# Decode attention on one core: the value product takes four cache rows per instruction in two column groups instead of two rows in four, for fourteen of sixteen V tiles

## The chip, the cores and the metric

The kernel runs on one core of a Trainium2 chip. Its time is the device time of one execution in microseconds (us); beside it stands the span of one profiled execution, from its first to its last instruction. Engines: PE (TensorE matmul; PEld is its weight load), DVE (VectorE), ACT (ScalarE), POOL (GpSimd), SP (SyncE, which here only issues DMAs). A line number like L491 is a line of the kernel.

## The reference

One decode step of a transformer block for 8 sequences, model width 512, float32 throughout. A modulation of six vectors per sequence comes from `silu(c) @ w_mod`. Attention has 32 query heads of width 128 over 8 cached heads, so 4 query heads share a K and a V; it sees the last 2048 of 8192 cached positions.

```python
W = min(4096, max(256, Sk // 4))                     # 2048
q = (x @ wq).reshape(B, Sq, Hq, Dh).transpose(0, 2, 1, 3)
k = repeat(k_cache[:, :, Sk - W:, :], 4, axis=1)
v = repeat(v_cache[:, :, Sk - W:, :], 4, axis=1)
p = softmax(einsum("bhqd,bhkd->bhqk", q, k) * Dh ** -0.5)
o = einsum("bhqk,bhkd->bhqd", p, v)
attention = o.transpose(0, 2, 1, 3).reshape(B, Sq, Hq * Dh) @ wo
...
h = layernorm(x) * (1 + ca) + sa
x = x + ga * attention(h)
h = layernorm(x) * (1 + cb) + sb
h = h @ w1 + b1;  h = max(h, 0) ** 2                 # 512 -> 1792
x = x + gb * (h @ w2 + b2)                           # 1792 -> 512
```

## The kernel before, in words

**Loads.** The cache is read once, in 32 tiles of 4 MB: K and V of each of 8 heads, each in two tiles. Together with the weights some 164 MB pass through SP's DMA queue, in an order written out by hand (`loads`): w_mod, wq, the first K tiles, then K tile n and V tile n - 2 in turn, with the pieces of `wo` between them, and at the end V14, V15, `tail` (the last of `wo` and half of w1), the rest of w1, and w2. There are four big slots in SBUF (`home`) and one small one. `load` gives a tile the slot that came free first; `done(key)` frees a slot after the last instruction that reads it, and `pump` then issues the next load.

**The loop.** All engines' instructions are put out in the order of the program (a manual schedule). The stage loop counts s from 0 to 37. Head g has four stages (i = s mod 4). A stage handles half a K tile, and half a V tile five stages behind (`PV_LAG`, v = s - 5). Its steps:

- `transposes` (L234, DVE): 32x32 blocks of K turned into `kT`, four calls a stage. `scores` (L405, PE): four instructions 32 outputs wide, one in each column group of TensorE, 512 columns each.
- `soft_a` to `soft_g`: when a head's scores are complete, the maximum (`mx`, a product with the identity in L421, `m`), a permutation by a product (`p_ps`, L436), the negative maximum (L441, `nm`), the exponential on ACT (L448), its multiplication by masks into `pr4` (L454 on ACT, L464 on DVE), and the transpose into `pT` (L471), which the value products use as weights. L477 (`pz`) sums the denominators.
- `weighted(v, h)` (L491, PE): a quarter of a V tile. V tile n covers one head hk and four of the eight sequences; its 16 KB per partition hold 64 cache rows j of 128 values. The weights are 16 columns for a row j (four sequences by four query heads). One instruction takes two rows, so 32 output partitions by 256 columns, of which the blocks with equal row on both sides are wanted; four instructions fill the four column groups, and twice that makes a quarter of the tile. Four quarters add up in one PSUM tile `o_ps`; the last of them frees the V tile.
- `parts(n)` (L508, L509, DVE): of the 2 x 2 blocks the wanted ones are picked by the masks `bit[4]` and added into `o_sb`, in two operations.
- `gather(hk)` (L526, PE, 64 outputs wide): the products with `pick` add up over partitions, put the heads in order, and DVE (L528, L532) writes them as columns to `oT`.
- `project_o(j)` (L544, PE): every second head, `wo` is applied to `oT` and added in `wo_ps`. For j = 0 and 1 one eighth of the rows of `wo` (the "far" rows, those whose index leaves 7 when divided by 8 and are not read with the others) comes by an indirect DMA in another order; there four products with `fsel` (L555), one for each r, bring the matching rows of `oT[:, 7]` into that order, ACT copies them to `oX`, and `far_rows` (L565) uses them four stages or so later.

The masks are made at the start from the identity: `bit[k]` is one bit of the partition number, `own` has four columns, one for each value of bits 2 and 3.

**The end.** After the last stage come `project_o(3)`, the residual and layer norm, w1 (L688), the squared ReLU, and w2 (L707), each waiting for its weights. `spin` (L643) puts products without a use on PE. In the last head's `soft_g` ACT issues five loads of the biases b1 and b2 (L580).

Of the kernel before, what the change touches and what calls it, by code (L numbers as in the profile page):

```python
# [8 lines left out]
F32 = mybir.dt.float32  # L9
AF = mybir.ActivationFunctionType  # L10
ALU = mybir.AluOpType
AX = mybir.AxisListType
# [8 lines left out]
def tile_adaln_cached_attention_mlp(  # L21
# [14 lines left out]
    nc = tc.nc  # L36
    P = 128
    B, HKV, SK, DH = k_cache.shape
# [15 lines left out]
    consts = ctx.enter_context(tc.tile_pool(name="consts", bufs=1))  # L54
    work = ctx.enter_context(tc.tile_pool(name="work", bufs=2))
# [10 lines left out]
    for q in range(D // P):  # L66
        b = slice(32 * q, 32 * q + B)
        nc.scalar.dma_start(xc_in[b], xc[b])

    ident = consts.tile([P, P], F32, name="ident")  # L70
# [2 lines left out]
    nc.gpsimd.memset(ones, 1.0)  # L73
    eps = consts.tile([P, 1], F32, name="eps")
    nc.vector.memset(eps, EPS)
    fsel = consts.tile([P, 4, P], F32, name="fsel")
    oX = consts.tile([P, 8, 32], F32, name="oX")
    pieces = consts.tile([P, 2], mybir.dt.int32, name="pieces")

# [2 lines left out]
    ways, n = [], 0  # L82
    for m, k in GROUPS:
        h, q = divmod(n, 4)
# [12 lines left out]
    nc.vector.tensor_copy(pieces[:, 0:1], pr_[:, 0:1])  # L97
    nc.vector.tensor_scalar(pieces[:, 1:2], pr_[:, 0:1], 2.0 * P, None, op0=ALU.add)
    nc.gpsimd.memset(fsel, 0.0)
    for to, h, q in ways:  # L100
        nc.gpsimd.tensor_copy(fsel[:, :, to], ident.rearrange("p (h r q) -> p r h q", h=8, r=4)[:, :, h, q])

# [76 lines left out]
    def slot(key, n, o=0):  # L181

        t = slots[size_of(key)][held[key]][:, o:]
        return t[:, : t.shape[1] // n * n].rearrange("p (a n) -> p a n", n=n)
# [16 lines left out]
    def done(*keys):  # L201
        for k in keys:
            free[size_of(k)].append(held.pop(k))
        pump()
# [39 lines left out]
    e = work.tile([P, P], F32, name="e_sb", tag="one_e_sb", bufs=1)  # L244
# [34 lines left out]
    h = work.tile([P, P], F32, name="h_sb", tag="one_h_sb", bufs=1)  # L279
# [5 lines left out]
    bit = {}  # L285
    for k in (2, 3, 4):
        n = 1 << k
        bit[k] = consts.tile([P, 2], F32, name=f"bit{k}")
        tmp = work.tile([P, 32 // n], F32, name=f"tmp{k}")
        nc.vector.tensor_reduce(tmp, sel[:, :32].rearrange("p (a n) -> p a n", n=n), axis=AX.X, op=ALU.add)  # L290
        nc.vector.tensor_reduce(bit[k], tmp.rearrange("p (a x) -> p x a", x=2), axis=AX.X, op=ALU.add)

    own = consts.tile([P, 4], F32, name="own")
    bq = consts.tile([P, B], F32, name="bq")
    for x in range(2):
# [16 lines left out]
    oT = consts.tile([P, 8, 32], F32, name="oT")  # L312
# [4 lines left out]
    for i, last in enumerate((16, 8)):  # L317
        at_ = 0
        while at_ < last:
            kc, m = divmod(16 * i + at_, 6)  # L320
            n = min(4 - m if m < 4 else 6 - m, last - at_)
            wv = slot(("mod", i), D)[:, at_ : at_ + n].rearrange("p m (q n) -> p m q n", q=NQ)
            for q in range(NQ):
# [4 lines left out]
                    start=(kc == 0),  # L328
                    stop=(kc == NQ - 1),
# [16 lines left out]
    for kc in range(NQ):  # L346
        w = slot(("wq", kc // 2), 512)[:, kc % 2 * 8 : kc % 2 * 8 + 8]
        for r in range(2):
            for g in range(4):
# [4 lines left out]
                    start=(kc == 0),  # L354
                    stop=(kc == NQ - 1),
# [21 lines left out]
    PT_, RZ_, RZP_, OS_, O_, MX_, SS_, X_ = {}, {}, {}, {}, {}, {}, {}, {}  # L377
# [90 lines left out]
    def soft_g(hk):  # L468
# [8 lines left out]
        nc.tensor.matmul(pz[b, :B], tsel.rearrange("p t d -> p (t d)"), RZP_.pop(hk), start=True, stop=True)  # L477
        nc.vector.reciprocal(RZ_[hk][b], pz[b, :B])

    def weighted(v, h):  # L480


        n, f = v // 2, 2 * (v % 2) + h
        hk, e = divmod(n, 2)
        vt = slot(("V", n), DH)
        if f == 0:
            O_[n] = ps_o.tile([P, 512], F32, name="o_ps")
        for x in range(2):
            for g in range(4):
                j = 16 * f + 8 * x + 2 * g  # L490
                nc.tensor.matmul(  # L491
                    O_[n][32 * g : 32 * g + 32, : 2 * DH],
                    PT_[hk][:, e, j : j + 2].rearrange("p j r -> p (j r)"),
                    vt[:, j : j + 2, :].rearrange("p j d -> p (j d)"),
                    start=(f == 0 and x == 0),
                    stop=(f == 3 and x == 1),
                )
        if f == 3:
            done(("V", n))

    def parts(n):

        hk, e = divmod(n, 2)
        o = O_.pop(n)
        if e == 0:
            OS_[hk] = work.tile([P, 2, P], F32, name="o_sb", bufs=1)
        d = OS_[hk][:, e, :]
        nc.vector.tensor_scalar(d, o[:, :DH], bit[4][:, 0:1], None, op0=ALU.mult)  # L508
        nc.vector.scalar_tensor_tensor(d, o[:, DH : 2 * DH], bit[4][:, 1:2], d, op0=ALU.mult, op1=ALU.add)  # L509

    def gather(hk):

# [25 lines left out]
    def project_o(j):  # L538

        last = j == HKV // 2 - 1  # L540
        key = ("tail", 0) if last else ("wo", j)
        w = slot(key, D)
        for i in range(8 if j > 1 else 7):
            nc.tensor.matmul(  # L544
                wo_ps[32 * (i % 4) : 32 * (i % 4) + 32, :],
                oT[:, i, :],
                w[:, i, :],
                start=(j == 0 and i < 4),
                stop=(last and i >= 4),
            )  # L550
        if j < 2:

            px = ps_m.tile([P, 512], F32, name="m_ps", tag="m_ps")
            for r in range(4):
                nc.tensor.matmul(px[:, 32 * r : 32 * r + 32], fsel[:, r], oT[:, 7, :], start=True, stop=True)  # L555
            px = px[:, :P].rearrange("p (r b) -> p r b", b=32)
            nc.scalar.copy(oX[:, :4], px)
        if not last:
            done(key)
# [26 lines left out]
    for s in range(N + PV_LAG + 1):  # L586
        g, i = divmod(s, C)
        q, h = divmod(s, 2)
# [15 lines left out]
        if v > C and v % (2 * C) == 1 and v < N:  # L604
            project_o(v // C // 2 - 1)
        if s in (18, 25):
            far_rows(s // 25)
        if 1 <= v <= N:
            weighted(v - 1, 1)
# [10 lines left out]
        if 1 <= v <= N and v % 2 == 0:  # L620
            parts(v // 2 - 1)
# [8 lines left out]
        if 0 <= v < N:  # L630
            weighted(v, 0)
        if ends:
            gather(v // C - 1)

    project_o(HKV // 2 - 1)


# [41 lines left out]
    for kc in range(NQ):  # L679
# [7 lines left out]
        for g in range(NQ):  # L687
# [4 lines left out]
                start=False,  # L692
                stop=(kc == NQ - 1),
# [3 lines left out]
    r = work.tile([P, FC, B], F32, name="relu", tag="a", bufs=1)  # L697
# [7 lines left out]
    for f in range(FC):  # L705
        for q in range(NQ):
# [4 lines left out]
                start=False,  # L711
                stop=(f == FC - 1),
            )
    y = work.tile([P, P], F32, name="y", tag="one_e_sb", bufs=1)
# [39 lines left out]
```

## Time and profile before

| | |
|---|---|
| time of three runs | 392.83, 392.85, 392.96 us; median 392.85 |
| profiled execution | span 390.9 us; its own time is not recorded beside it, the runs' median is 1.95 us longer |
| PE busy | 260.2 us (67%), of it L405 129.0 us, L491 68.5 us |
| DVE busy | 224.2 us (57%), of it L234 151.4 us |
| HBM read | 166.24 MB, 425 GB/s over the span |
| granted TensorE clock | 0.900 of full speed, mean |

A matmul in float32 shows as two records in the trace, so the 512 instructions of L491 count as 1024. A row of the timeline has start, duration, engine, line, operation, tile written <- tiles read, shape, count, and in brackets the engine's idle time before it and what ended that. Several rows of PE overlap, because a record lasts until its modelled end; the time that a step takes is read from start to start. A row of the windows view has busy time and count for each engine, then the granted clock (PEclk), the DMA engines' busy share and the GB/s.

### The profile page before, as it was taken

The numbers are of one execution on the slowest core, as the hardware profiler recorded it, in microseconds if no ns is written. First come the engines' busy times: TensorE is split into PE (matmuls) and PEld (weight loads), VectorE is DVE, ScalarE is ACT, GpSimd is POOL, SyncE is SP. The second block draws the span as 40 slices with busy tenths as digits, with TensorE's granted clock in tenths as the row PEclk, the third lists the DMA queues.
The fourth block names the chain that finished last, engine by engine and source line by source line (L and its number), as shares of the span: only waits on it lengthen the run. The fifth ranks groups of instructions, "written<-read, shape, count | busy, mean of one in ns | idle before, by whom it ended". The sixth has DMA issues, their size and how long they took to land.

```text
span 390.9 us, 4829 instructions
## 1 busy us (share of the span) xinstructions
PE 260.2 (67%) x2066; PEld 81.8 (21%) x2066; DVE 224.2 (57%) x316; ACT 46.7 (12%) x91; POOL 10.2 (3%) x36
## 2 busy tenths in 40 slices
PE   0080958868337973798379737783788237996895
PEld 0030211112011321242113212321222011322433
DVE  1360099879057935775579457391789057855231
ACT  0120011221003100310031003100201003004010
POOL 4000000000000000030000000200000000000000
PEclk9997789999859996999599969989799859998999
DMA  8999999999999999999999999999999999999995
GB/s 330 431 436 423 434 443 436 438 426 403 441 429 429 431 433 433 431 438 419 431 424 433 431 443 423 428 433 428 433 428 419 443 436 428 425 433 420 416 433 224
DMA packets 7157, 165.04 MB, mean 422 GB/s; under 512 B 1016, under 2 KB 1184, under 8 KB 1440
## 3 DMA queue, kind: packets, MB, share of 16 engines
q1 hardware_dynamic: 6768, 164.17, 98.1%
q0 software_dynamic: 288, 0.53, 0.4%
q8 instruction: 16, 0.26, 0.3%
q10 hardware_dynamic: 80, 0.04, 0.0%
q14 instruction: 5, 0.04, 0.0%
HBM read 166.24 MB, written 0.07 MB: 425 GB/s over the span
## 4 chain that ended last, share of the span: by engine, by line
DMA 53%; DVE 23%; PE 18%; issue 5%; ACT 1%; SPq 0%; ACTq 0%; DVEq 0%
DMA home<-in_A_k_cache_dram 37%; DVE kT L234 12%; DMA home<-in_A_wq_dram 9%; PE s_ps L405 6%; DMA home<-in_B_w_dram 5%; DVE pT L471 5%; PE p_ps L436 3%; PE o_ps L491 3%; PE m_ps L350 2%; DVE pr L464 2%; DMA pr<-in_B_b_dram 2%; DVE mx L419 1%; PE m_ps L421 1%; DVE qbd L368 1%; PE m_ps L441 1%
## 5 line engine op out<-in xcount | busy, mean ns | idle before, releaser
L234 DVE STREAM_TRANSPOSE kT<-home 128x1024 f32<-128x1024 f32 x128 | 151.4, 1220 | 79.7 <-DMA home<-in_A_k_cache_dram 75.8
L405 PE MATMUL s_ps<-kT,qst 128*32 128x512 f32 x512 | 129.0, 1075 | 12.2 <-DVE kT L234 11.9
L491 PE MATMUL o_ps<-home,pT 128*32 128x256 f32 x1024 | 68.5, 390 | 10.8 <-DVE pT L471 10.5
L491 PEld LDWEIGHTS o_ps<-home,pT 128*32 128x32 f32 x1024 | 33.2, 115 | 101.1 <-issue 57.8
L421 PE MATMUL m_ps<-ident,mx 128*1 128x128 f32 x16 | 4.3, 364 | 63.8 <-DVE mx L419 63.8
L405 PEld LDWEIGHTS s_ps<-kT,qst 128*32 128x32 f32 x512 | 14.1, 114 | 30.5 <-DVE kT L234 22.4
L471 DVE STREAM_TRANSPOSE pT<-pr 128x2048 f32<-128x2048 f32 x8 | 18.3, 2281 | 1.0 <-ACT pr L454 1.0
L454 ACT ACTIVATE pr<-pr,own 128x512 f32<-128x512 f32 x16 | 17.8, 1225 | 0.3
L448 ACT ACTIVATE pr<-p_ps,nm 128x512 f32<-128x512 f32 x8 | 5.5, 688 | 102.7 <-DVE nm L445 102.7
L350 PE MATMUL m_ps<-home,oX 128*32 128x512 f32 x64 | 9.5, 757 | 9.8 <-DMA home<-in_A_wq_dram 9.8
L415 ACT COPY ss<-s_ps 128x512 f32<-128x512 f32 x8 | 4.7, 586 | 90.5 <-issue 62.4
L421 PEld LDWEIGHTS m_ps<-ident,mx 128*1 128x1 f32 x16 | 0.7, 81 | 69.0 <-DVE mx L419 69.0
L393 ACT COPY qst<-q_ps 32x128 f32<-32x128 f32 x32 | 8.2, 257 | 52.2 <-PE q_ps L382 52.0
L368 DVE COPY qbd<-m_ps 32x128 f32<-32x128 f32 x8 | 3.0, 373 | 18.8 <-PE m_ps L365 18.7
L436 PE MATMUL p_ps<-ss,perm 128*128 128x512 f32 x16 | 12.9, 896 | 0.0
L445 DVE TENSOR_SCALAR nm<-m_ps 128x1 f32<-128x1 f32 x8 | 1.3, 159 | 17.5 <-PE m_ps L441 17.5
L268 PE MATMUL m_ps<-xsum,sel 128*128 128x1 f32 x2 | 0.6, 363 | 15.5 <-DVE xsum L266 15.5
L526 PE MATMUL m_ps<-o_sb,pick 128*64 128x224 f32 (+2 forms) x48 | 9.9, 345 | 0.9 <-DVE o_sb L509 0.9
L154 POOL MEMSET small<- 128x2048 f32 x2 | 3.6, 1802 | 240.8 <-PE wo_ps L544 240.8
L464 DVE TENSOR_SCALAR pr<-pr,own 128x512 f32<-128x512 f32 x16 | 9.2, 661 | 0.8 <-ACT pr L448 0.8
L528 DVE STREAM_TRANSPOSE tr<-m_ps 64x512 f32<-64x512 f32 x8 | 5.7, 714 | 5.5 <-PE m_ps L526 5.2
L508 DVE TENSOR_SCALAR o_sb<-o_ps,bit 128x128 f32<-128x128 f32 x16 | 5.3, 329 | 4.7 <-PE o_ps L491 4.5
(139 smaller groups left out, 137.7 us busy)
## 6 DMA issues: line engine op xcount, KB each, us to landing
home<-in_A_k_cache_dram SPq DMA_DIRECT2D x16, 4096.0 KB, 31.1
home<-in_A_v_cache_dram SPq DMA_DIRECT2D x15, 4096.0 KB, 20.6
home<-in_w_mod_dram SPq DMA_DIRECT2D x1, 4096.0 KB, 12.7
home<-in_A_v_cache_dram SPq DMA_DIRECT2D x2, 2048.0 KB, 19.5
small<-in_A_wo_dram SPq DMA_DIRECT2D x2, 1792.0 KB
small<-in_w_mod_dram SPq DMA_DIRECT2D x1, 2048.0 KB
small<-in_A_wo_dram SPq DMA_DIRECT2D x1, 2048.0 KB
home<-in_A_wo_dram SPq DMA_DIRECT2D x1, 2048.0 KB, 14.6
```

The lines of the kernel that those rows point to most:

```text
L234: nc.vector.transpose(KTS[q, j][:, rows], k[:, rows, 32 * j : 32 * j + 32])
L350: nc.tensor.matmul(pqs[r][32 * g : 32 * g + 32, :], hT[:, kc, :], w[:, 4 * r + g, :], start=(kc == 0), stop=(kc == NQ - 1),)
L368: nc.vector.tensor_copy(qbd[b, 4 * r : 4 * r + 4, j].rearrange("p g (b t) -> p t g b", t=REP), pT_[b].rearrange("p (t g b) -> p t g b", t= ...
L393: nc.scalar.copy(own[b, :, :, i, 0], pq[b, :P].rearrange("p (c m t) -> p c m t", c=2, t=REP))
L405: nc.tensor.matmul(s_ps[0][32 * g : 32 * g + 32, :], qst[hk % 2][:, P * (4 * c + u) + 32 * j :][:, :32], kT[:, u], start=(c == 0 and j == ...
L421: nc.tensor.matmul(MX_[hk][0:1, :P], mx, ident, start=True, stop=True)
L436: nc.tensor.matmul(sp, perm, SS_.pop(hk), start=True, stop=True)
L454: nc.scalar.mul(X_[hk][..., w], pr, own[:, w : w + 1])
L464: nc.vector.tensor_scalar(X_[hk][..., w], pr, own[:, w : w + 1], None, op0=ALU.mult)
L471: nc.vector.transpose(PT_[hk].rearrange("p e j r -> p j e r"), X_.pop(hk).rearrange("p j x w -> p j (x w)"))
L491: nc.tensor.matmul(O_[n][32 * g : 32 * g + 32, : 2 * DH], PT_[hk][:, e, j : j + 2].rearrange("p j r -> p (j r)"), vt[:, j : j + 2, :].rear ...
L526: nc.tensor.matmul(dest, pick[:, x].rearrange("p t u -> p (t u)"), src, start=True, stop=True)
```

## The change

For V tiles 0 to 13 (`at_once(n)` is 4, for 14 and 15 it stays 2) an instruction of `weighted` takes four cache rows: 64 output partitions by 512 columns, in two column groups of 64. A quarter of a tile is then four instructions instead of eight. Of the 4 x 4 blocks four are wanted, so `parts` uses four masks (`jrow`) and four DVE operations instead of two. The PSUM tile is the same, used in its whole width.

For the far rows, `fsel` no longer has a matrix for each r: it is one 128 x 128 matrix, and `oT[:, 7]` is first copied into four column blocks, each multiplied by the mask of its r (`own`, DVE, into `o7`). One product with 128 columns replaces four with 32. At the start, two reductions for `jrow` and one for `rows_of` are added on DVE, and POOL's copies into `fsel` are a quarter as wide.

```diff
-    fsel = consts.tile([P, 4, P], F32, name="fsel")
+    fsel = consts.tile([P, P], F32, name="fsel")
...
+    rows_of = consts.tile([P, 8, 4], F32, name="rows_of")
+    nc.vector.tensor_reduce(rows_of, ident.rearrange("p (h r q) -> p h q r", h=8, r=4), axis=AX.X, op=ALU.add)
     for to, h, q in ways:
-        nc.gpsimd.tensor_copy(fsel[:, :, to], ident.rearrange("p (h r q) -> p r h q", h=8, r=4)[:, :, h, q])
+        nc.gpsimd.tensor_copy(fsel[:, to], rows_of[:, h, q])
...
+    jrow = consts.tile([P, 4], F32, name="jrow")
+    tmp = work.tile([P, 8], F32, name="tmpj")
+    nc.vector.tensor_reduce(tmp, ident.rearrange("p (a n) -> p a n", n=16), axis=AX.X, op=ALU.add)
+    nc.vector.tensor_reduce(jrow, tmp.rearrange("p (a x) -> p x a", x=4), axis=AX.X, op=ALU.add)
...
+    def at_once(n):
+        return 4 if n < 2 * HKV - 2 else 2
...
+        a = at_once(n)
         for x in range(2):
-            for g in range(4):
-                j = 16 * f + 8 * x + 2 * g
+            for g in range(8 // a):
+                j = 16 * f + 8 * x + a * g
                 nc.tensor.matmul(
-                    O_[n][32 * g : 32 * g + 32, : 2 * DH],
-                    PT_[hk][:, e, j : j + 2].rearrange("p j r -> p (j r)"),
-                    vt[:, j : j + 2, :].rearrange("p j d -> p (j d)"),
+                    O_[n][16 * a * g : 16 * a * (g + 1), : a * DH],
+                    PT_[hk][:, e, j : j + a].rearrange("p j r -> p (j r)"),
+                    vt[:, j : j + a, :].rearrange("p j d -> p (j d)"),
...
-        nc.vector.tensor_scalar(d, o[:, :DH], bit[4][:, 0:1], None, op0=ALU.mult)
-        nc.vector.scalar_tensor_tensor(d, o[:, DH : 2 * DH], bit[4][:, 1:2], d, op0=ALU.mult, op1=ALU.add)
+        row_of = jrow if at_once(n) == 4 else bit[4]
+        nc.vector.tensor_scalar(d, o[:, :DH], row_of[:, 0:1], None, op0=ALU.mult)
+        for x in range(1, at_once(n)):
+            nc.vector.scalar_tensor_tensor(
+                d, o[:, x * DH : (x + 1) * DH], row_of[:, x : x + 1], d, op0=ALU.mult, op1=ALU.add
+            )
...
-            for r in range(4):
-                nc.tensor.matmul(px[:, 32 * r : 32 * r + 32], fsel[:, r], oT[:, 7, :], start=True, stop=True)
+            o7 = work.tile([P, 2, 2, 32], F32, name="o7", bufs=1)
+            nc.vector.tensor_mul(
+                o7,
+                oT[:, 7, None, None, :].to_broadcast([P, 2, 2, 32]),
+                own.rearrange("p (x y) -> p y x", x=2)[..., None].to_broadcast([P, 2, 2, 32]),
+            )
+            nc.tensor.matmul(px[:, :P], fsel, o7.rearrange("p y x b -> p (y x b)"), start=True, stop=True)
```

## The prediction

> **What bounds the kernel now.** I read the page first, then the DMA queue's issues and waits, then the timeline of PE and DVE in the loop and at its end, and the clock by stages.
>
> ```profile
> PE 260.2 (67%) x2066; PEld 81.8 (21%) x2066; DVE 224.2 (57%) x316; ACT 46.7 (12%) x91; POOL 10.2 (3%) x36
> DMA  8999999999999999999999999999999999999995
> DMA 53%; DVE 23%; PE 18%; issue 5%; ACT 1%; SPq 0%; ACTq 0%; DVEq 0%
> ```
>
> The DMA engines are busy in every slice but the first and the last: the stream of loads is the bound, and no engine is. So compute costs nothing while two things hold: slots come free before the stream runs dry, and the work behind the last landings isn't late. The first I read from one head's period, from the landing of one even K tile to the next.
>
> ```profile
> core 0: us, PE busy (x) PEld busy (x) DVE busy (x) ACT busy (x) POOL busy (x), PEclk, DMA share, GB/s
> 189.23:228.55 39.32, 28.25 (x218) 8.64 (x218) 25.54 (x31) 4.62 (x9) 0.00 (x0) 0.89 1.01 433
> ...
> 221.52 1.09 PE L491 MATMUL o_ps<-home,pT 128*32 128x256 f32 x16
> ...
> 228.55 2.37 DVE L234 STREAM_TRANSPOSE kT<-home 128x1024 f32<-128x1024 f32 x2 [9.33 <-DMA home<-in_A_k_cache_dram]
> 316.51 2.37 DVE L234 STREAM_TRANSPOSE kT<-home 128x1024 f32<-128x1024 f32 x2 [14.24 <-DMA home<-in_A_k_cache_dram]
> ...
> 327.88 6.48 SPq L131 DMA_DIRECT2D home<-in_A_v_cache_dram  x2
> 335.86 6.99 DVE L234 STREAM_TRANSPOSE kT<-home 128x1024 f32<-128x1024 f32 x6 [0.74 <-DMA home<-in_A_k_cache_dram]
> ```
>
> In a period of 39.32 us PE works 28.25, is done at 222.6, and DVE then waits 9.33 for the next K tile; K14's landing at 316.51 ends a longer wait, 14.24. V13's load goes out at 327.88, as soon as V11's last product is done, but its turn on the DMA engines comes only when K15 has landed, about 335.9: 8.0 us of slack there.
>
> The second I read from the end.
>
> ```profile
> 354.22 0.25 PE L477 MATMUL m_ps<-zs,tsel 128*64 128x8 f32 x2 [0.58 <-DVE zs L466]
> 357.43 1.86 PE L491 MATMUL o_ps<-home,pT 128*32 128x256 f32 x16 [2.95 <-DVE pT L471]
> 359.22 1.93 PE L526 MATMUL m_ps<-o_sb,pick 128*64 128x256 f32 x4
> 361.08 6.25 PE L491 MATMUL o_ps<-home,pT 128*32 128x256 f32 x112
> ...
> 380.74 1.98 PE L643 MATMUL q_ps<-ident 128*128 128x512 f32 x4
> 383.58 1.96 PE L707 MATMUL m_ps<-home,pr 128*32 128x128 f32 x64 [0.85 <-DMA home<-in_B_w_dram]
> 385.97 1.73 PE L707 MATMUL m_ps<-home,pr 128*32 128x128 f32 x48 [0.44 <-DMA home<-in_B_w_dram]
> ```
>
> From K14's landing to the output there is one long chain of compute beside the stream: softmax of the last two heads, the products of V12 to V15, the output projection, the MLP. It meets the stream again at the last product (L707), which waits for w2 0.85 and 0.44 us. So the chain is only a little early. The spins end at 382.72 as modelled, about 382.5 as the next row would begin; 64 records take 1.96, so 112 take about 3.3, and without a wait PE would be done at 385.8 instead of 387.70. **Slack at the end: 1.9 us.** That is what the change may spend behind K14.
>
> **The change part by part.**
>
> *The product of one quarter V tile* (`weighted`, L491). Before: 8 instructions of 256 columns, 32 outputs wide, so two in each of four column groups. After, for V0 to V13: 4 instructions of 512 columns, 64 wide, so two in each of two groups.
>
> ```profile
> 323.66 1.07 PE L491 MATMUL o_ps<-home,pT 128*32 128x256 f32 x16
> 324.66 0.38 PE L441 MATMUL m_ps<-ones,m 1*128 1x1 f32 x2
> ...
> 332.02 1.07 PE L491 MATMUL o_ps<-home,pT 128*32 128x256 f32 x16 [1.08 <-DVE pT L471]
> 333.02 1.08 PE L526 MATMUL m_ps<-o_sb,pick 128*64 128x256 f32 x4
> ...
> 335.82 1.92 PE L544 MATMUL wo_ps<-small,oT 128*32 128x512 f32 x16
> 337.56 1.04 PE L491 MATMUL o_ps<-home,pT 128*32 128x256 f32 x16
> 338.42 1.98 PE L405 MATMUL s_ps<-kT,qst 128*32 128x512 f32 x8
> 340.20 1.06 PE L491 MATMUL o_ps<-home,pT 128*32 128x256 f32 x16
> 341.09 1.99 PE L405 MATMUL s_ps<-kT,qst 128*32 128x512 f32 x8
> 342.89 1.06 PE L491 MATMUL o_ps<-home,pT 128*32 128x256 f32 x16
> ...
> 345.69 1.07 PE L491 MATMUL o_ps<-home,pT 128*32 128x256 f32 x16
> 346.55 2.01 PE L405 MATMUL s_ps<-kT,qst 128*32 128x512 f32 x8
> 348.34 1.08 PE L491 MATMUL o_ps<-home,pT 128*32 128x256 f32 x16
> 350.04 0.38 PE L421 MATMUL m_ps<-ident,mx 128*1 128x128 f32 x2 [0.61 <-DVE mx L419]
> ```
>
> Start to start the old product takes 0.88 (340.20 to 341.09). L544 streams two 512-column instructions through each of its groups, as the new product will, and takes 1.74 (335.82 to 337.56). It has as many records as the old product (16) and takes twice as long: columns per group set the pace, not the number of instructions. Bounds: 0.44, if half the records meant half the time; about 3.9, if two 64-wide groups did not run side by side (the spins, one stream, take 1.98 for 4 records; here 8). I take 1.74, the row with the same stream per group: **+0.86 per product.** No row has two 64-wide groups at once. The Trainium skill, "TensorEngine Tiling (Array Packing)", Tiling Modes, lists 128x64 as two independent tiles; no run so far shows it.
>
> *Change of width.* Followed by an instruction of the same width (L405) the old product takes 0.88, by one of another (L441, L526) 1.00: 0.12 for a change. The scores stay 32 wide, so a new product between two of them has two changes: 1.74 + 0.24 = 1.98, +1.10. Bounds: 0 and 0.25 each. The Trainium skill, same page, Key Properties, says that a change of tiling mode drains TensorE, which speaks against this change; it gives no time, and the 0.12 agrees. Without that price the sum below would be 1.0 lower.
>
> *Adding the rows up* (`parts`): two more DVE operations for each of 14 tiles.
>
> ```profile
> L509 DVE SCALAR_TENSOR_TENSOR o_sb<-o_ps,bit,o_sb 128x128 f32<-128x128 f32 x16 | 5.6, 351 | 0.6
> ...
> 169.54 4.62 DVE L234 STREAM_TRANSPOSE kT<-home 128x1024 f32<-128x1024 f32 x4 [1.13 <-DMA home<-in_A_k_cache_dram]
> ...
> 169.11 1.92 PE L544 MATMUL wo_ps<-small,oT 128*32 128x512 f32 x14
> 170.96 1.08 PE L555 MATMUL m_ps<-oT,fsel 128*128 128x32 f32 x8
> 171.97 1.07 PE L491 MATMUL o_ps<-home,pT 128*32 128x256 f32 x16
> ```
>
> 2 x 0.35 = 0.70 each, 9.8 in all, in DVE's idle time but for V11 and V13 below.
>
> *Far rows* (`project_o`, twice). Four products (1.01, 170.96 to 171.97) become one, at most 0.38 (L421 has its size), but that waits for a new DVE multiplication (0.35, as L509), queued on DVE behind the first two transposes of an odd K tile (169.54 to 171.9). PE's queue stands meanwhile: the product of a V tile, and through it that tile's release. About 172.7 instead of 172.0, so +0.7 twice (bounds: -0.6, and a late K tile's wait), long before the end; the 8 us of DVE's wait for K covers it. The two setup reductions and the smaller POOL copies lie under the first weight loads; nothing.
>
> *The loop.* Per head the eight products cost PE at most 8 x 1.10 = 8.8. PE would be done at 222.6 + 8.8 = 231.4. What follows on it, L421 for the next head, needs the next K tile's first two transposes (228.55 + 2.37 = 230.9) and a maximum behind them, so it can't come before 231 anyway: it just fits, and the longer wait before K14 clears any rest. A V slot is released 2 us later at 327.88, against 8.0 of slack, so the stream stays whole. The cover is nearly used up: PE's idle time is gone, and any more would move K's release.
>
> *The end.* From K14's landing: the product at 323.66 stands ahead of L441, on which the exponential and pT wait: +0.86. The one at 332.02 is followed by 64-wide L526, so it loses one change: 1.00 to 1.74, +0.74; the two DVE additions (0.70) run beside it. Those at 337.56, 340.20, 342.89 and 345.69 stand in a closed row of PE work: 4 x 1.10 = 4.40. The one at 348.34 had 1.70 until L421 and needs 1.86 to 1.98: +0.2. Both of V13's lie beside the softmax. Sum **6.2**, until pT.
>
> Then a gain. The product at 357.43 and L526 took 3.65 for work that takes 2.0 elsewhere, because the clock had dropped.
>
> ```profile
> 358.00:361.00 3.00, 3.00 (x17) 0.97 (x8) 0.35 (x1) 0.00 (x0) 0.00 (x0) 0.50 1.02 427
> 361.00:364.00 3.00, 3.00 (x57) 1.81 (x60) 0.98 (x3) 0.00 (x0) 0.00 (x0) 1.00 1.01 428
> ...
> 363.31 3.52 SPq L136 DMA_DIRECT2D home<-in_B_w_dram  x4
> ...
> SPq L136 <- DMA pr<-in_B_b_dram: 4.3, 5, 1.6
> ```
>
> PE was idle 2.95 before, with almost nothing (0.25) in the 0.6 before that. V13's two products now last 1.7 longer, so the gap shrinks to about 1.8, between the 1.08 without a drop (332.02) and the 2.95 with one. The Trainium skill, "TensorE: Matmul & The Clock Gate", What's actually happening, has half rate after an idle window of about 3.4 us, free-running; that agrees with the drop here. By it a gap of 1.8 keeps the clock; the sum with a drop would be 0.9 higher. I take no drop. Then L526 waits for V13's four DVE operations instead, and comes at the same distance from pT, but takes 1.0 instead of 1.86: -0.9. **Late by 5.3**, against 1.9 of slack: +3.4. The last weight loads, w2's from 363.31, wait for the bias loads issued behind pT, so they go out some 6 us later; the tail's two pieces (2.1 and 1.8 MB by their shapes) stand ahead of them, 9 us at 430 GB/s. The stream ends when it did; without that cover the end would come up to 6 us later.
>
> The span is 390.9 and the median 392.85, so 1.95 lies around it. 392.85 + 3.4 = 396.25; I say **396.2**.
>
> **The rivals.** *No change, the other side.* The new product takes about as long as the old (0.9 to 1.2, if two wide groups stream faster than L544's four). Then the end is late by some 1.6 at most, under the 1.9, and the time is 392.9: DMA sets it. It decides below a cost of about 0.3 per product. For it: DVE and PE are busy 57% and 67% of the span, under a full stream. Against it: L544's 1.74.
>
> *Wide groups one after another.* A product takes 3.4 to 3.9: +2.6 at least, 20.8 per head on an active part of 33.4 (189.23 to 222.6), so 54 against 39.3. PE is then the bound for seven heads: +15 each, some 105, time 495.
>
> *Faster.* The denser PE keeps its clock and the product is covered; but the end is then w2's landing, 387.3 at the earliest. It needs a faster stream: half a per cent more than some 430 GB/s would be 2 us, 391. The rates of 427 to 433 in the rows above allow for that, and nothing in the change causes it.
>
> **How the numbers follow.** Slower by the end's chain 0.74; its own range is 395.0 (no price for a change of width: 5.3 less 1.0) to 398.3 (0.25 for each change, +1.2, and the clock drops, +0.9). No change 0.14; groups in turn 0.06; faster 0.06. A difference under 0.2% (0.8 us) can't be told from none here. The range 392.7 to 398.3 holds the first two, 0.88. Slower 0.80, same 0.14, faster 0.06.
>
> **What would show it.** After: L491's wide records, 8 per product, in about 1.74; the scores' start-to-start around them 0.24 longer; DVE's waits for K little changed at K10 and K14; PE's idle time before K10 near nothing; DMA in nines; L707 not waiting for w2, its last records ending some 3.4 us after w2's landing plus 0.5; a granted clock near 1.00 after pT of the last head. Wrong if L707 still waits for w2 (then the product was cheap), or if DMA shows holes in the loop (then slots came late).

## The result and the profile after

The changed kernel takes 397.75 us (396.96 to 397.86, 4 runs) against 392.84 (392.66 to 392.96): ratio 1.0122, 95% interval 1.0109 to 1.0134, so **slower by 4.9 us**. The profiled run took 397.78 with a span of 396.0. One of the ten runs of first12, further down, took 816.0 us at a granted clock of 1.00; the record doesn't explain it, and the ratio leaves it out.

The page of the changed kernel, its window over the same period of the loop, and PE's and DVE's timelines there:

```profile
PE 310.7 (78%) x1606; PEld 76.1 (19%) x1606; DVE 236.0 (60%) x349; ACT 46.8 (12%) x91; POOL 9.7 (2%) x36
DMA  8999999999999999999999999999999999999990
DMA 44%; PE 28%; DVE 24%; issue 4%; SPq 0%; ACT 0%; DVEq 0%; ACTq 0%
...
189.23:228.55 39.32, 36.09 (x162) 7.83 (x158) 27.30 (x35) 5.02 (x10) 0.00 (x0) 1.00 1.01 433
...
226.28 1.94 PE L503 MATMUL o_ps<-home,pT 128*64 128x512 f32 x8
231.44 0.48 PE L428 MATMUL m_ps<-ident,mx 128*1 128x128 f32 x2 [3.22 <-DVE mx L426]
...
228.44 2.37 DVE L236 STREAM_TRANSPOSE kT<-home 128x1024 f32<-128x1024 f32 x2 [5.07 <-DMA home<-in_A_k_cache_dram]
316.54 2.37 DVE L236 STREAM_TRANSPOSE kT<-home 128x1024 f32<-128x1024 f32 x2 [10.72 <-DMA home<-in_A_k_cache_dram]
```

The stream of loads is as whole as before: 9 in every slice between the first and the last, 433 GB/s in the period, K10 landing at 228.44 (228.55 before) and K14 at 316.54 (316.51). PE is busy 50 us longer, and nothing of that shows in the loop: the waits for K have shrunk (9.33 to 5.07, 14.24 to 10.72) and PE still idles 3.22 before K10's maximum. But the chain that ended last has shifted from DMA (53% to 44%) towards PE (18% to 28%), and the last slice has a 0 for DMA where it had a 5: the stream is over, and compute ends the kernel.

The end, from K14's landing on (lines have moved: L441 is L448, L526 L542, L421 L428, L477 L484, L491 L503, L405 L412, L544 L560, L707 L728; in the variants further down they move by a few more):

```profile
325.72 0.38 PE L448 MATMUL m_ps<-ones,m 1*128 1x1 f32 x2
334.87 1.03 PE L542 MATMUL m_ps<-o_sb,pick 128*64 128x256 f32 x4
...
339.46 1.94 PE L503 MATMUL o_ps<-home,pT 128*64 128x512 f32 x8
341.33 1.99 PE L412 MATMUL s_ps<-kT,qst 128*32 128x512 f32 x8
343.25 1.94 PE L503 MATMUL o_ps<-home,pT 128*64 128x512 f32 x8
...
354.60 1.94 PE L503 MATMUL o_ps<-home,pT 128*64 128x512 f32 x8
356.46 0.38 PE L428 MATMUL m_ps<-ident,mx 128*1 128x128 f32 x2
361.63 0.23 PE L484 MATMUL m_ps<-zs,tsel 128*64 128x8 f32 x2
361.89 2.31 DVE L478 STREAM_TRANSPOSE pT<-pr 128x2048 f32<-128x2048 f32 x1 [1.39 <-PE m_ps L484]
364.26 1.56 PE L503 MATMUL o_ps<-home,pT 128*32 128x256 f32 x16 [2.40 <-DVE pT L478]
366.03 1.97 PE L542 MATMUL m_ps<-o_sb,pick 128*64 128x256 f32 x4 [0.21 <-DVE o_sb L523]
367.93 6.32 PE L503 MATMUL o_ps<-home,pT 128*32 128x256 f32 x112
387.66 1.98 PE L664 MATMUL q_ps<-ident 128*128 128x512 f32 x4
389.58 3.26 PE L728 MATMUL m_ps<-home,pr 128*32 128x128 f32 x112
```

Read against the same rows of before, the lateness grows like this:

| step | before | after | late by |
|---|---|---|---|
| L441, negative maximum of head 6 | 324.66 | 325.72 | 1.06 |
| L526, gather of head 5 | 333.02 | 334.87 | 1.85 |
| V13's second product, behind the last scores | 348.34 | 354.60 | 6.26 |
| L421, maximum of head 7 | 350.04 | 356.46 | 6.42 |
| first product behind pT | 357.43 | 364.26 | 6.83 |
| the row of seven products | 361.08 | 367.93 | 6.85 |
| spins before w2 | 380.74 | 387.66 | 6.92 |
| PE's end | 387.70 | 392.84 | 5.14 |

The last product no longer waits for w2: its 112 records run in one piece of 3.26. The 6.92 of lateness became 5.14 of time, so 1.78 was slack.

### The profile page after: what moved, and what is told of

It reads as the page before. It is cut to its first block, busy times and chain, and to the rows that moved or that the text cites. A ratio compares the mean times of both kernels' runs of the same rounds, so it can differ in the third digit from the quotient of the medians.

```text
span 396.0 us, 3942 instructions
## 1 busy us (share of the span) xinstructions
PE 310.7 (78%) x1606; PEld 76.1 (19%) x1606; DVE 236.0 (60%) x349; ACT 46.8 (12%) x91; POOL 9.7 (2%) x36
## 4 chain that ended last, share of the span: by engine, by line
DMA 44%; PE 28%; DVE 24%; issue 4%; SPq 0%; ACT 0%; DVEq 0%; ACTq 0%
DMA home<-in_A_k_cache_dram 35%; DVE kT L236 12%; DMA home<-in_A_wq_dram 9%; PE o_ps L503 9%; PE s_ps L412 7%; DVE pT L478 5%; PE p_ps L443 3%; PE m_ps L357 2%; DVE o_sb L523 2%; DVE pr L471 2%; DVE mx L426 1%; PE q_ps L664 1%; PE m_ps L542 1%; PE wo_ps L560 1%; PE m_ps L709 1%
## 5 line engine op out<-in xcount | busy, mean ns | idle before, releaser
L412 PE MATMUL s_ps<-kT,qst 128*32 128x512 f32 x512 | 128.4, 1074 | 5.1 <-DVE kT L236 5.1
L503 PE MATMUL o_ps<-home,pT 128*64 128x512 f32 (+1 forms) x576 | 118.0, 566 | 9.4 <-DVE pT L478 9.4
L503 PEld LDWEIGHTS o_ps<-home,pT 128*64 128x64 f32 (+1 forms) x576 | 31.5, 133 | 131.6 <-issue 106.4
L428 PE MATMUL m_ps<-ident,mx 128*1 128x128 f32 x16 | 3.8, 324 | 28.3 <-DVE mx L426 28.3
L412 PEld LDWEIGHTS s_ps<-kT,qst 128*32 128x32 f32 x512 | 11.4, 112 | 37.4 <-DVE kT L236 19.0
L523 DVE SCALAR_TENSOR_TENSOR o_sb<-o_ps,jrow,o_sb 128x128 f32<-128x128 f32 x42 | 14.7, 351 | 1.5
L443 PE MATMUL p_ps<-ss,perm 128*128 128x512 f32 x16 | 12.0, 843 | 0.0
L542 PE MATMUL m_ps<-o_sb,pick 128*64 128x224 f32 (+2 forms) x48 | 9.8, 342 | 1.1 <-DVE o_sb L523 1.1
L544 DVE STREAM_TRANSPOSE tr<-m_ps 64x512 f32<-64x512 f32 x8 | 5.7, 714 | 4.5 <-PE m_ps L542 4.3
L426 DVE TENSOR_REDUCE mx<-s_ps 128x1 f32<-128x512 f32 x8 | 5.3, 661 | 4.2 <-ACT ss L422 4.2
```

The costliest lines, as they stand in the source:

```text
L412: nc.tensor.matmul(s_ps[0][32 * g : 32 * g + 32, :], qst[hk % 2][:, P * (4 * c + u) + 32 * j :][:, :32], kT[:, u], start=(c == 0 and j == ...
L426: nc.vector.tensor_reduce(mx, s_ps[0], axis=AX.X, op=ALU.max)
L443: nc.tensor.matmul(sp, perm, SS_.pop(hk), start=True, stop=True)
L503: nc.tensor.matmul(O_[n][16 * a * g : 16 * a * (g + 1), : a * DH], PT_[hk][:, e, j : j + a].rearrange("p j r -> p (j r)"), vt[:, j : j + a ...
L523: nc.vector.scalar_tensor_tensor(d, o[:, x * DH : (x + 1) * DH], row_of[:, x : x + 1], d, op0=ALU.mult, op1=ALU.add)
L542: nc.tensor.matmul(dest, pick[:, x].rearrange("p t u -> p (t u)"), src, start=True, stop=True)
```

## The experiments

**Where in the kernel the loss arises.** Two kernels, the wide product for one part of the tiles each.

```diff
-        return 4 if n < 2 * HKV - 2 else 2
+        return 4 if n < 2 * HKV - 4 else 2                       # first12
+        return 4 if 2 * HKV - 4 <= n < 2 * HKV - 2 else 2        # last2
```

> Wide product for V0 to V11 alone; V12 and V13 go back to two rows per instruction. Theory (the loss is PE's row of work behind K14's landing, products of V11 to V13, less the slack of 1.8 us at the end): only V11's last two products are wide behind K14, so the last head's pT comes some 1.2 us later, less than the slack: 392.9 us. Rival (the loss comes from the loop: slots freed later, holes in the stream, twelve fourteenths of the wide products): 397.0 us.

> Wide product for V12 and V13 alone. Theory (end of the kernel): all of the loss but V11's share of 0.9 us: 396.9 us. Rival (loop): two fourteenths of the loss: 393.5 us.

first12: 392.81 us, ratio 1.0004 (0.9994 to 1.0014). last2: 397.91 us (396.07 to 398.56), ratio 1.0138 (1.0121 to 1.0155). Twelve of the fourteen wide tiles by themselves cost nothing, though V11's last two products lie behind K14: the maximum of head 7 comes at 351.24 instead of 350.04, and these 1.20 stay under the slack. The other two tiles cost, by the medians, as much as all. The loop is out. last2 is 1.0 over its forecast, and its four runs lie 2.5 apart. Part of that lies outside the span: the spans are 394.1, 395.5, 395.9 and 395.8 (395.2 to 396.1 for the changed kernel), and two of the four times stand 2.7 above theirs, where the changed kernel's stand 1.8 above. Its profiled run is the one of 396.07:

```profile
319.56 0.37 PE L428 MATMUL m_ps<-ident,mx 128*1 128x128 f32 x1 [13.84 <-DVE mx L426]
321.93 1.12 PE L443 MATMUL p_ps<-ss,perm 128*128 128x512 f32 x2
322.98 1.07 PE L503 MATMUL o_ps<-home,pT 128*32 128x256 f32 x16
354.70 0.38 PE L428 MATMUL m_ps<-ident,mx 128*1 128x128 f32 x2
```

Here p_ps was over in 1.05 (321.93 to 322.98); in the changed kernel it took 1.96 (321.89 to 323.85), at half clock. That 0.9 and V11's 0.87 (its product takes 1.00 until 323.98, in the changed kernel 1.87 until 325.72) make L428 of head 7 1.76 earlier than the changed kernel's 356.46. The other three runs, with no trace, were slower; why they exceed 396.9 stays open.

**The rest of the change by itself.** The change with `at_once` always 2, and for V0 to V13 two more DVE operations in `parts`:

```diff
+        if n < 2 * HKV - 2:
+            d2 = work.tile([P, P], F32, name="d2", bufs=1)
+            for x in range(2):
+                nc.vector.scalar_tensor_tensor(d2, o[:, x * DH : (x + 1) * DH], row_of[:, x : x + 1], d, op0=ALU.mult, op1=ALU.add)
```

> All that the change does but the wide product: the far rows by one product with masked right-hand sides, the masks at the start, and for V0 to V13 two further DVE operations of the same size behind the two (into a tile that nobody reads). Theory: DVE has the idle time, 392.9 us. Rival (the additions and the far rows' wait take part in the loss): 393.6 us or more; V13's additions alone lie on the path to the output and are worth 0.7 us there.

392.73 us, ratio 1.0004 (0.9994 to 1.0013). None of this costs anything. The far rows' wait is there, but covered:

```profile
172.57 0.46 PE L579 MATMUL m_ps<-o,fsel 128*128 128x128 f32 x2 [1.29 <-DVE o L574]
```

One thing this run doesn't test: its further additions write a tile that nobody reads, so V13's gather doesn't wait for them. In the changed kernel it must, which is 0.69 of idle time in keep_clock's rows below. half_columns, next, has the additions on the path.

**Columns or width.** The changed form has twice the columns per group and, against the scores, a change of width. Two kernels have one of them each.

```diff
 half_columns: 64 wide, 256 columns (four additions read the two blocks in turn)
-                    O_[n][16 * a * g : 16 * a * (g + 1), : a * DH],
+                    O_[n][16 * a * g : 16 * a * (g + 1), : 2 * DH],
-                    vt[:, j : j + a, :].rearrange("p j d -> p (j d)"),
+                    vt[:, j : j + 2, :].rearrange("p j d -> p (j d)"),
 double_columns: 32 wide, 512 columns
...
+                m = min(j, 60) if a == 4 else j
                 nc.tensor.matmul(
+                    O_[n][32 * g : 32 * g + 32, : a * DH],
+                    PT_[hk][:, e, j : j + 2].rearrange("p j r -> p (j r)"),
+                    vt[:, m : m + a, :].rearrange("p j d -> p (j d)"),
```

> The wide product with 256 columns instead of 512: 64 wide, two groups, the same number of instructions, half of the columns left out (so half of the wanted blocks are missing), four DVE operations as in the change. Theory (columns per group set the pace, a change of width costs 0.12 us): the product lasts 0.9 and 1.1 between two score products, the last head's pT is late by some 1.3 us, under the slack: 392.9 us. Rival (the 64-wide form itself, its weight loads or the drain at each change of width, is what costs): product stays near 1.9, 397 us.

> Products of V0 to V13 stay 32 wide in four groups, eight instructions a quarter, but each streams 512 columns as the changed kernel's do (the further columns give blocks that nobody wants, so the output isn't the reference's); four DVE operations as in the change. No change of width against the scores. Theory: 1.74 a product, the scores' 1.78 as before; pT of the last head some 1.0 to 1.3 us earlier than in the changed kernel (two changes of width saved at four or five products): 396.6 us. Rival (width costs nothing here, columns all): 397.7 us.

half_columns: 392.91 us, ratio 1.0009 (1.0000 to 1.0019). PE's timeline in the row of products and scores without a pause (337 to 348 us before):

```profile
337.98 1.08 PE L503 MATMUL o_ps<-home,pT 128*64 128x256 f32 x8
338.99 1.98 PE L412 MATMUL s_ps<-kT,qst 128*32 128x512 f32 x8
340.91 1.08 PE L503 MATMUL o_ps<-home,pT 128*64 128x256 f32 x8
```

double_columns: 397.58 us, ratio 1.0118 (1.0101 to 1.0135). The same place:

```profile
341.44 1.98 PE L412 MATMUL s_ps<-kT,qst 128*32 128x512 f32 x8
343.23 1.91 PE L504 MATMUL o_ps<-home,pT 128*32 128x512 f32 x16
344.96 1.98 PE L412 MATMUL s_ps<-kT,qst 128*32 128x512 f32 x8
...
360.95 2.31 DVE L478 STREAM_TRANSPOSE pT<-pr 128x2048 f32<-128x2048 f32 x1 [1.37 <-PE o_ps L504]
363.32 1.07 PE L504 MATMUL o_ps<-home,pT 128*32 128x256 f32 x16 [2.28 <-DVE pT L478]
365.09 1.89 PE L543 MATMUL m_ps<-o_sb,pick 128*64 128x256 f32 x4 [0.70 <-DVE o_sb L524]
```

Start to start, product and scores (256 columns from the kernel before and half_columns, 512 from double_columns and the changed kernel):

| | 32 wide | 64 wide |
|---|---|---|
| 256 columns | 0.88, 1.78 | 1.01, 1.92 |
| 512 columns | 1.73, 1.79 | 1.87, 1.92 |

Columns cost 0.86, a change of width 0.13 on either side, and the two add up. Two groups 64 wide do run side by side: one after another, four streams of 256 columns at 0.43 (half of L544's 0.87 for 512) would take 1.7, not 1.01. The columns are what slows the kernel: the width alone stays under the slack. double_columns has its pT 0.94 before the changed kernel's, about as forecast, but its time of 397.58 is the rival's 397.7, not the forecast 396.6. Its clock drop lay later (granted clock 0.50 from 366 to 368 and 0.85 to 370 us), over part of the seven products: they began 1.02 earlier (366.91 for 367.93), took 7.07 instead of 6.32, and the gather behind them was only 0.26 earlier (374.85 for 375.11).

**The clock drop behind the last scores.** Two spins behind the last L484:

```diff
+        if hk == HKV - 1:
+            gap = ps_1.tile([P, 512], F32, name="q_ps").rearrange("p (a n) -> p a n", a=4)
+            for _ in range(2):
+                nc.tensor.matmul(gap, ident, ident[:, None, :].to_broadcast([P, 4, P]), start=True, stop=True)
```

> The changed kernel with two spins (products without a use, 1.7 us) on PE behind the last head's L484, in the gap of 2.4 us before pT. Theory (the granted clock drops in that gap, so the product behind pT and L542 take 1.56 and 1.97 instead of 1.0 and 1.1): the clock stays at 1.00, L542 begins with the last DVE addition as before and ends 0.9 us sooner: 396.9 us, as the one run of the changed kernel that took 396.96. Rival (those two are slow for another reason): 397.75 us.

396.25 us (395.94 to 396.75), ratio 1.0085 (1.0068 to 1.0102). First two windows of the changed kernel, then one of keep_clock and its PE timeline:

```profile
364.00:366.00 2.00, 1.56 (x16) 0.51 (x16) 1.82 (x6) 0.00 (x0) 0.47 (x1) 0.68 1.00 422
366.00:368.00 2.00, 1.97 (x8) 0.82 (x12) 0.00 (x0) 0.00 (x0) 0.00 (x0) 0.50 1.01 429
```

```profile
364.00:366.00 2.00, 1.28 (x17) 0.61 (x18) 1.61 (x5) 0.00 (x0) 0.47 (x1) 1.00 1.00 422
...
361.56 1.98 PE L489 MATMUL q_ps<-ident 128*128 128x512 f32 x4
364.03 1.07 PE L507 MATMUL o_ps<-home,pT 128*32 128x256 f32 x16 [0.49 <-DVE pT L478]
365.79 1.08 PE L546 MATMUL m_ps<-o_sb,pick 128*64 128x256 f32 x4 [0.69 <-DVE o_sb L527]
366.80 6.25 PE L507 MATMUL o_ps<-home,pT 128*32 128x256 f32 x112
```

With PE busy in the gap the clock stays, and L546 takes 1.01 instead of L542's 1.90. From pT to the seven products it is 5.14 (361.66 to 366.80) instead of 6.04 (361.89 to 367.93): the 0.9 forecast. The time falls by more, 1.5 by the medians; 0.2 of the profiled run's gain had arisen before the spins (its pT began at 361.66), and where the rest comes from isn't shown. In the changed kernel the clock reads 1.00 up to 364, 0.85 in the next microsecond and 0.50 from 365 to 368: it fell only when PE was at work again, not in the gap itself.

**The wait for the old pT.** The last head's pT in the query buffers, which are read out by then:

```diff
+        if hk == HKV - 1:
+            PT_[hk] = qst_all[:, :, : B * P].rearrange("p e (j r) -> p e j r", r=16)
```

> The changed kernel, but the last head's pT lies in a buffer of its own (the query buffers, which are read out by then), so that its transpose doesn't wait until V13's products have read the old pT. Theory: pT begins when ACT is done, 0.4 us earlier: 397.35 us, or 396.5 if the shorter gap of PE (2.0 us) also keeps the clock. Rival (the transpose waits for something else): 397.75 us.

> Both of these at once: pT in a buffer of its own and two spins in the gap. Theory: the two savings add up, 0.4 + 0.9: 396.45 us. What then remains over the kernel before, 3.6, is V11's to V13's products (5.4 by pT) less the slack of 1.8.

own_pT: 397.17 us (396.83 to 399.63), ratio 1.0106 (1.0089 to 1.0123). Its profiled run is the slowest of them, so only its DVE row is used; below it stands the row of the kernel before:

```profile
361.56 2.31 DVE L482 STREAM_TRANSPOSE qst<-pr 128x2048 f32<-128x2048 f32 x1 [1.02 <-ACT pr L462]
...
355.06 2.31 DVE L471 STREAM_TRANSPOSE pT<-pr 128x2048 f32<-128x2048 f32 x1 [0.99 <-ACT pr L454]
```

The transpose waits for ACT now, as it did before the change, and starts 5.07 behind head 7's maximum (L429, 356.49) instead of 5.43: the 0.4 is there. In the time it can't be told: the median fell by 0.6, but the ranges overlap (by span, four runs of 394.6 to 395.4 and one of 397.5 against 395.2 to 396.1). The shorter gap on PE, 2.03, didn't keep the clock in the profiled run, where it read 0.50 from 365 to 371. both_gaps with 396.32 (395.61 to 397.35), ratio 1.0098 (1.0080 to 1.0116) is no better than keep_clock. Its forecast of 396.45 was met, the sum of two savings not shown.

**The slack by itself.** In the kernel before, `spin(1)` behind the output projection becomes `spin(5)`.

> The kernel before with four more spins (4 x 0.86 = 3.45 us of PE) behind the output projection, in the chain to the last product. Measures the slack at the end by itself. Theory (1.8 us of slack against w2's landing): + 1.65, 394.5 us. Rival (no slack, any delay counts in full): 396.3 us; (more slack than thought, the stream ends it): 392.9 us.

395.01 us (394.21 to 395.67), ratio 1.0050 (1.0033 to 1.0067), 0.5 over the forecast. From PE's timeline:

```profile
369.47 1.08 PE L526 MATMUL m_ps<-o_sb,pick 128*64 128x256 f32 x4 [0.87 <-DVE o_sb L509]
374.84 4.56 PE L643 MATMUL q_ps<-ident 128*128 128x512 f32 x10
385.46 1.98 PE L643 MATMUL q_ps<-ident 128*128 128x512 f32 x4
387.37 3.26 PE L707 MATMUL m_ps<-home,pr 128*32 128x128 f32 x112
```

This run was 1.28 late ahead of the spins already (L526 at 369.47, 368.19 in the first profile): the clock stayed at 0.50 until 363, where the first profile has 1.00 from 361, and the seven products took 7.25 instead of 6.25. It was 4.72 late at the last spins (385.46 for 380.74). PE ends at 390.63 instead of 387.70, 2.93 late: 1.79 of slack, the changed kernel's 1.78 again.

**All sixteen tiles.** `at_once` is 4 throughout.

> The wide product for all sixteen V tiles. Theory: V14's and V15's eight products lie in a closed row behind pT, beside nothing; each takes 0.87 more (no change of width between them), and each tile's two further DVE operations come on top where PE or DVE waits for them (V15's, 0.7): 397.75 + 7.0 + 0.7 = 405.4 us. Rival (they still wait for V15's landing, so part is hidden): 401 us or less.

405.59 us (404.80 to 406.48), ratio 1.0334 (1.0317 to 1.0351). The eight products behind pT cost in full, as forecast; V15's landing hides none of it.

**Both gaps filled, a misjudged one.** keep_clock's two spins, and 16 or 28 spins before K14's landing:

```diff
+        if s == N - 4:
+            cold = ps_1.tile([P, 512], F32, name="q_ps").rearrange("p (a n) -> p a n", a=4)
+            for _ in range(16):                                  # last2_warm: 28
+                nc.tensor.matmul(cold, ident, ident[:, None, :].to_broadcast([P, 4, P]), start=True, stop=True)
```

> The changed kernel with PE kept busy in both of its last long gaps: 16 spins (6.9 us) before K14's landing and two behind the last L484. It takes the chance of a clock drop out of the comparison. Theory: p_ps behind K14 takes 1.05 instead of 1.96 (0.9 us gained), the work behind pT another 0.9: 397.75 - 1.8 = 395.95 us. Rival (the drops cost nothing, only the columns do): 397.75 us.

> Wide product for V12 and V13 alone, with PE kept busy in the same two gaps (28 spins before K14's landing, since PE is done sooner, and two behind the last L484). Theory: last2 came out 1.0 us over its forecast because the clock dropped more in its longer gaps; without drops it stands below after_warm by V11's product, 0.87: 395.1 us. Rival (V11's product costs nothing, V12 and V13 make up the whole loss, as the medians of last2 and the changed kernel say): 395.95 us.

402.09 us, ratio 1.0238 (1.0221 to 1.0255), and 405.11, ratio 1.0315 (1.0298 to 1.0332): both forecasts missed. I had counted 0.43 us for a spin, which is one of its two records.

```profile
310.52 14.00 PE L638 MATMUL q_ps<-ident 128*128 128x512 f32 x32
324.46 0.27 PE L428 MATMUL m_ps<-ident,mx 128*1 128x128 f32 x1
360.23 0.38 PE L428 MATMUL m_ps<-ident,mx 128*1 128x128 f32 x2
```

```profile
329.94 0.27 PE L428 MATMUL m_ps<-ident,mx 128*1 128x128 f32 x1
364.82 0.38 PE L428 MATMUL m_ps<-ident,mx 128*1 128x128 f32 x2
...
332.00:345.00 13.00, 10.97 (x71) 3.27 (x74) 9.58 (x14) 3.01 (x4) 0.00 (x0) 1.00 0.65 265
```

The first rows are after_warm's, the others last2_warm's. Sixteen spins lasted 14.00 and held L428 until 324.46, 4.9 late. The times say nothing of the theories; two stretches do. From one L428 to the next head's, both at full clock, it is 35.77 in after_warm and 34.88 in last2_warm: V11's product costs 0.89, and V12 and V13 are not the whole loss. And in last2_warm, L428 some 10 us late, the stream runs dry: 0.65 busy, 265 GB/s over 13 us. In after_warm, 4.9 late, the same window has only a small dip: 0.95 and 387, against 1.01 and 436 in the changed kernel. V13's load went out at 337.32 in last2_warm and at 333.68 in after_warm, 9.4 and 5.8 behind the 327.88 of the kernel before; the slot slack, put at 8.0, lies between.

No version ran faster than the kernel before; first12, others_only and half_columns can't be told apart from it.

## Why the prediction was right

Right in sign, mechanism and range (396.2 in 392.7 to 398.3; measured 397.75); the loss came out as 4.9 where 3.4 was forecast. The range held because its upper end allowed 0.9 for a clock drop; without that it would have ended at 397.4. By its steps:

- *Product, 0.86 more, and 0.12 for each change of width.* 1.87 against 0.88, beside scores 0.13 longer: 0.86 and 0.13. L544, the row with the same stream per group, was the right price.
- *The loop hides it.* So it did (first12). The estimate was too cautious: PE kept 3.22 of idle time instead of nothing. Two things in the traces make up most of that. PE idles 1.81 instead of 8.00 before the maximum at the start of the period, and the clock, 0.50 from 189 to 196 us in the kernel before, is 1.00 there now, so that p_ps takes 1.06 (194.73 to 195.79) instead of 2.01 (194.57 to 196.58). And the second product of a head lies in a wait of 0.94 that PE had anyway (before L477 at 201.93).
- *Far rows +0.7.* From L544's start to the next product it took 2.86 before and 3.59 in others_only (169.37 to 172.96): the forecast, to 0.03. In the changed kernel it took 2.40 (170.89 to 173.29), a gain of 0.46: PE comes there 1.8 later, when DVE has done its multiplication. Without weight either way.
- *Sum 6.2 until pT.* 6.42 at L421.
- *"Both of V13's lie beside the softmax."* This step failed. pT has one buffer; its transpose overwrites what V13's products read, and waited for them: 1.39 of idle time, released by PE, where own_pT's waits 1.02 for ACT. From 6.42 the lateness grew to 6.83: 0.4, shown by own_pT's row.
- *"I take no drop", -0.9.* This failed too. The gap was 2.40, not 1.8, in part through the wait just told, and the clock went to 0.50; the work behind pT took 3.67, as before (3.65). Nor would 1.8 have been safely short, as own_pT's 2.03 shows. keep_clock shows the gain that was counted on, once something keeps PE busy. The Trainium skill, "TensorE: Matmul & The Clock Gate", What's actually happening, on which the choice leaned, speaks of an idle window of about 3.4 us; here a gap of 2.40 was enough, so the page's window can't mean 3.4 us without any work, and the measurement decides. The drop before the change, which the prediction took to agree with the page, stood behind a gap of 2.95 and said so already. "The sum with a drop would be 0.9 higher" was the right branch.
- *Slack 1.9.* 1.78, and 1.79 in before_late.
- *w2's loads some 6 us later, under cover.* They went out at 369.86 instead of 363.31, and L728 doesn't wait for them.

So 6.2 - 0.9 - 1.9 = 3.4 became 6.92 - 1.78 = 5.14 in the profiled run: 0.9 more for the clock, 0.4 for pT, 0.3 in the rest of the lateness and 0.1 less slack. Two side sums are off without weight: the lower end of its own range comes out at 395.25 by its terms, not 395.0, and the groups in turn at 498, not 495. Of the rivals, "no change" needed a product under some 0.3 more; half_columns is that case, and it is the same as before. "Groups one after another" is refuted by 1.87. The stream was no faster.

## What to carry to other kernels

In a kernel bound by its stream of loads, a price per step says little until it is put at a place: the same product is free in the loop and costs in full behind the last K landings (V12, V13 and one product of V11), because there the compute chain has only 1.8 us to spare. Measure that spare time first, from the waits of the last instructions for the last loads, and price a change only along the chain that leads there. And look for reuse of buffers: work "beside" a chain is on it as soon as a single buffer ties the two.

## What the runs showed of the hardware

- In the changed kernel a gap of 2.40 us on PE, after 29 us without a pause (333.10 to 361.86), brought the granted clock to 0.50 for some 3 us, beginning about half a microsecond after PE had resumed (364.26); 2.03 in own_pT did too, while gaps of 1.08 before pT of the earlier head did not. How long the drop lasts differs between runs whose code at that place is the same: the seven products behind it took 6.25 in the kernel before and 7.25 in before_late.
- The kernels that compute ends scattered more than the one that the stream ends: by span the kernel before lay within 390.7 and 391.1 in 25 runs, last2 within 394.1 and 395.9 in 4. The clock takes part: of the changed kernel's runs, the three of 397.72 to 397.86 had a mean granted clock of 0.930, the one of 396.96 had 0.951. That it is the whole reason isn't shown.
- A change between 32 and 64 output columns costs 0.13 us on each side, the scores' included. The Trainium skill, "TensorEngine Tiling (Array Packing)", Key Properties, says that it drains TensorE, without a time; no run here shows the drain by itself, only this price.
